# Column vectors through small TensorE transposes, filter loads into the Z tiles, a third hn buffer and late column sums in a spectral-gating and MLP block with its backward pass

## The chip, the cores and the metric

The kernel runs on one core of a Trainium2 chip. The metric is device time in microseconds (us). The engines are called PE (TensorE, with PEld for its weight loads), DVE (VectorE), ACT (ScalarE), POOL (GpSimd) and SP (SyncE); SP issues all of the kernel's DMAs, in its own program order.

## The reference

The reference computes one transformer-like block and, through its vector-Jacobian product, all its gradients. S = 2048 rows, D = 512 columns, F = 1792 hidden columns, bf16:

```python
mod = (silu(c) @ w_mod)           # sa, ca, ga, sb, cb, gb: six rows of 512
h = layernorm(x) * (1 + ca) + sa
x = x + ga * irfft2(rfft2(h) * (w_r + 1j * w_i))
h = layernorm(x) * (1 + cb) + sb
out = x + gb * (relu(h @ w1 + b1) ** 2 @ w2 + b2)
_out, _vjp = jax.vjp(_f, A_x, A_w_r, A_w_i, B_w1, B_b1, B_w2, B_b2, c, w_mod)
_grads = _vjp(grad_out)
```

The ten outputs are `out` (out_0) and the gradients of x (out_1), of the filter `w_r`, `w_i` (out_2, out_3; 2048 x 257 each), of w1 (out_4), b1 (out_5), w2 (out_6), b2 (out_7), c (out_8) and w_mod (out_9).

## The kernel before

Rows are held as 128 partitions by 16 row tiles `t` (four blocks `b` of four). The two-dimensional Fourier transforms are products with tables built on the chip: LF and LG (stored to DRAM and loaded again for the backward pass as LFb, LGb), Cf, CdF, CdB and TA. A spectrum is worked on in eight pairs `gi`, each a tile of 128 x (2, 2, 257).

The stages, in order of the program:

1. **Start.** x, c, w_mod and transposed loads of grad_out (gT) and w2 arrive. c lands as a 128 x 4 column tile `ccol` (L532) and b1 as a 128 x 14 column tile `b1colb` (L548); both are read from DRAM so that neighbouring elements of a partition lie 128 elements apart. Layernorm statistics, the first transform, the six modulation rows, the tables. In the background, `gaT = w2 · grad_out` (L640).
2. **Forward spectrum** (L656 to L672). `spec_f23` makes a pair's spectrum X; `ew_f` multiplies it with the filter pair (`Wt[gi]`, a ring of three tiles named W) into `Z[gi]` and stores X to `xs_dram`. `spec_g1` and `spec_g23` transform Z back.
3. **MLP forward and backward to its input** (`stage_g`, `stage_h`, `stage_o`, L721 to L854). `stage_h` makes h and gaT and stores both to DRAM (`h_dram`, `gh_dram`). `stage_o` makes the output rows, and the gradient rows `u` (two buffers), each stored to `gx1_dram` and transformed into UT for the backward spectrum. The gradient of b1, `gb1b`, a 128 x 14 column tile, is then written twice: to out_5 and to `gb1_dram` (L852 to L854), every element to its own place of 2 bytes.
4. **Backward spectrum** (L937 to L955). The same transforms; `ew_b` multiplies the gradient G with the filter (`Wb`, two buffers) into Z, and with the stored spectrum (`Xb`, two buffers) into gW, the filter's gradient (two buffers), which goes to out_2 and out_3. In `spec_f23` ACT copies one half of each AE tile and DVE the other (L357, L358).
5. **Rows of the gradient of x** (L962 to L1002). For each of the 16 row tiles: `spec_g23` on PE, copies on ACT, eight instructions on DVE, the store of `gx`. `n1b` and `gxb` bring four row tiles at a time. Two column sums on PE per row tile (L982 with `gh1`, L983 with `q1`) run four rows late (`Delayed(4)`).
6. **Weight gradients.** `grad_w1` (L888): seven transposed loads `ghn` from gh_dram (two buffers), 64 matmuls L900 for each, in groups of 16 that end in three DVE instructions (L903, L909, L912). `grad_w2` (L876): fourteen transposed loads `hn` from h_dram (two buffers), 16 matmuls L882 each. `GMod.emit` makes a row block of the gradient of w_mod; each call needs a load `wmc` (one buffer). The gradient of c, `gcb`, a 128 x 4 column tile, goes to out_8 (L1024), again 2 bytes to a place.

The order on each engine is set by the framework's scheduler from the order of the code and from priorities. `Priority(tc, LATE)` around grad_w1, grad_mod_mid and grad_w2 puts their instructions behind those of the later stage 5 where both could run, so that grad_w1 fills gaps of PE in stage 5 and runs alone behind it, and grad_w2 comes last. Each engine then takes its instructions in that fixed order, and so does SP with its DMAs: a DMA that has to wait holds back all that stand behind it on SP.

Of the kernel before, what the change touches and what calls it, by code (L numbers as in the profile page):

```python
# [9 lines left out]
AF = mybir.ActivationFunctionType  # L10
# [75 lines left out]
def build_ta(tc, K, constp, g, pspool):  # L86
# [17 lines left out]
    pst = pspool.tile([P, P], BF16, name="ta_ps")  # L104
# [218 lines left out]
def spec_f23(tc, K, UT, Cd, dc, dest, elementwise):  # L323

    nc = tc.nc
    with tc.tile_pool(name="aep", bufs=1) as aep, \
# [18 lines left out]
        for gi in range(8):  # L345
# [12 lines left out]
            nc.vector.tensor_copy(out=dst[:, 1], in_=src[:, 1])  # L358
# [99 lines left out]
def kernel(  # L458
# [92 lines left out]
    nc.vector.tensor_copy(ccolf, ccol)  # L551
# [8 lines left out]
    psF1 = tc.alloc_tile_pool(name="psF1", bufs=2, space=PSUM)  # L560
    psM = tc.alloc_tile_pool(name="psM", bufs=2, space=PSUM)
# [138 lines left out]
    with tc.tile_pool(name="psR", bufs=1, space=PSUM) as psR, tc.tile_pool(name="psO", bufs=2, space=PSUM) as psO_pool, \  # L700
# [151 lines left out]
        with nc.allow_non_contiguous_dma(reason="tiny"):  # L852
            nc.sync.dma_start(out5_view, gb1b)
            nc.sync.dma_start(gb1_dram.rearrange("(fc p) -> p fc", p=P), gb1b)  # L854
# [82 lines left out]
    with tc.tile_pool(name="f23b", bufs=2) as fr, tc.tile_pool(name="ewb", bufs=2) as ew:  # L937
        Wt, Xt = [], []
        for gi in range(8):
            Wt.append(fr.tile([P, 2, 2, FP], BF16, name="Wb"))  # L940
            nc.sync.dma_start(Wt[gi][:, :, 0, 0:DF], wr_view[:, pair_slice(gi), :])
            nc.sync.dma_start(Wt[gi][:, :, 1, 0:DF], wi_view[:, pair_slice(gi), :])
# [3 lines left out]
        def ew_b(gi, G):  # L946
            cmul(nc, ew, Wt[gi], G, Z[gi][:, :, 0, 0:DF], Z[gi][:, :, 1, 0:DF], True)
# [14 lines left out]
    with tc.tile_pool(name="fin", bufs=2) as fp, tc.tile_pool(name="psE", bufs=2, space=PSUM) as psE, \  # L962
# [3 lines left out]
        late = Delayed(4)  # L966
        for b in range(NB):
            n1b = fp.tile([P, TB, D], BF16, name="n1b")
            nc.sync.dma_start(n1b, n1_dram[:, TB * b:TB * b + TB, :])
            gxb = fp.tile([P, TB, D], BF16, name="gxb")  # L970
            nc.sync.dma_start(gxb, gx1_dram[:, TB * b:TB * b + TB, :])
            for j in range(TB):
                t = TB * b + j
                n1row = n1b[:, j, :]
                psY = spec_g23(tc, K, CS, t, fp, psE, psE)
                gh1 = fp.tile([P, D], BF16, name="gh1", bufs=6)
                nc.scalar.copy(out=gh1, in_=psY)
                q1 = fp.tile([P, D], BF16, name="q1", bufs=6)
                nc.vector.tensor_tensor(q1, gh1, n1row, op=ALU.mult)

                def sums(t=t, gh1=gh1, q1=q1):
                    nc.tensor.matmul(gsa_ps, lhsT=K["ones_col"], rhs=gh1, start=(t == 0), stop=(t == NT - 1))  # L982
                    nc.tensor.matmul(gca_ps, lhsT=K["ones_col"], rhs=q1, start=(t == 0), stop=(t == NT - 1), tile_position=(0, 32))  # L983

                late.add(sums)
                gn = fp.tile([P, D], BF16, name="gn")
                nc.vector.tensor_tensor(gn, gh1, modb[:, CA1_B, :], op=ALU.mult)
                rr = fp.tile([P, 4], FP32, name="rr")
                gs = fp.tile([P, D], BF16, name="gs")
                nc.scalar.activation(gs, gn, AF.Copy, scale=inv1[:, t:t + 1], accum_out=rr[:, 0:1])  # L990
                jk = fp.tile([P, D], BF16, name="jk1")
                nc.vector.scalar_tensor_tensor(out=jk, in0=gs, scalar=K["onef"], in1=n1row, op0=ALU.mult, op1=ALU.mult,  # L992
                                               accum_out=rr[:, 1:2])
                nc.vector.tensor_scalar(rr[:, 2:4], rr[:, 0:2], -1.0 / D, None, op0=ALU.mult)
                v = fp.tile([P, D], BF16, name="v")
                nc.vector.tensor_scalar(v, n1row, rr[:, 3:4], rr[:, 2:3], op0=ALU.mult, op1=ALU.add)
# [67 lines left out]
```

## Time and profile before

| | us |
|---|---|
| median of 3 runs | 629.2 |
| lowest and highest | 621.39 and 630.54 |
| the profiled execution | 626.75 |
| its span on the core | 624.9 |
| PE busy, of the span | 499.5 (80%) |
| DVE busy | 402.2 (64%) |
| ACT busy | 239.0 (38%) |
| mean granted clock of TensorE | 0.924 of full speed |

Times in the profile are microseconds from the start of the span. A row of the timeline gives the start, the busy time, the engine, the line, the operation, the output and the inputs, and in square brackets the idle time ahead of it with what ended that. A row of the table of stretches gives the stretch, its length, the busy time (and number) of PE, PEld, DVE, ACT and POOL, the granted clock of TensorE, the mean busy share of the 16 DMA engines and the GB/s that they moved. A row of a DMA issue gives output, input, count, KB of each and the median us from issue to landing. Busy times of matmuls are modelled ends of pipelined instructions, so rates are taken from start to start or over whole rows.

### The profile page before, as it was taken

To read this page: it belongs to the slowest core of one execution; us is meant where nothing else is said; L and a number is where in the kernel's file an instruction comes from. 1 tells how busy PE (TensorE), PEld (TensorE's weight loads), DVE (VectorE), ACT (ScalarE), POOL (GpSimd) and SP (SyncE) were. 2 spreads that over 40 slices of the span, in tenths; PEclk is the share of its full clock that TensorE was granted. 3 is DMA by queue.
4 is the path that set the end of the run, shared out by engine and by line. 5 is a ranking of instruction groups with operands and counts; after the bars stand their busy time and mean duration, and the time that the engine had idled before them with its cause. 6 is when DMAs were issued, how large, how long until landed. Compare 5 with 4: busy or idle time off the path is not lost.

```text
span 624.9 us, 8582 instructions
## 1 busy us (share of the span) xinstructions
PE 499.5 (80%) x2803; PEld 256.5 (41%) x2844; DVE 402.2 (64%) x1133; ACT 239.0 (38%) x415; POOL 30.1 (5%) x112
## 2 busy tenths in 40 slices
PE   0778999989879989899999409767796499987666
PEld 0523468633433333344443104435442288732222
DVE  5897977375695895783794224976489977645001
ACT  2656854454522352253451104324476222251000
POOL 3212000022000011000000000000000000000000
PEclk9799999999989999989999858888999599989769
DMA  8963677364864374564289877999984189489654
GB/s 304 205 199 131 195 158 199 108 198 140 224 206 144 102 250 152 149 210 150 69 285 179 32 163 242 261 217 233 226 249 140 53 179 184 81 235 258 51 102 111
DMA packets 168096, 108.96 MB, mean 174 GB/s; under 512 B 94322, under 2 KB 162164, under 8 KB 167156
## 3 DMA queue, kind: packets, MB, share of 16 engines
q1 hardware_dynamic: 168052, 108.42, 68.6%
q8 instruction: 22, 0.36, 0.2%
q14 instruction: 22, 0.18, 0.1%
HBM read 43.02 MB, written 44.92 MB: 141 GB/s over the span
## 4 chain that ended last, share of the span: by engine, by line
DMA 20%; PE 20%; DVE 12%; SPq 3%; issue 2%; ACT 0%; POOL 0%; DVEq 0%; ACTq 0%; POOLq 0%
DMA hn<-h_dram 7%; PE mm L900 5%; PE mm L882 5%; DMA gx_dram<-u 5%; DMA out_dram<-gW 3%; PE og L781 3%; PE mm L763 2%; DMA ghn<-gh_dram 2%; PE og L799 2%; SPq L895 2%; DVE p L408 1%; DVE gaT L770 1%; DVE p L409 1%; DMA Wb<-in_A_w_r_dram 1%; DVE jk L992 1%
## 5 line engine op out<-in xcount | busy, mean ns | idle before, releaser
L882 PE MATMUL mm<-g_sb,hn 128*128 128x512 bf16 x219 | 58.1, 421 | 19.4 <-DMA hn<-h_dram 19.0
L640 PE MATMUL mm<-gT,w2T 128*128 128x512 bf16 x217 | 54.4, 378 | 8.3 <-DVE gaT L643 5.7
L900 PE MATMUL mm<-ghn,n_sb 128*128 128x256 bf16 x448 | 54.6, 282 | 7.5 <-DVE gw L912 5.1
L781 PE MATMUL og<-w,h 128*128 128x512 bf16 x217 | 55.9, 386 | 3.6 <-DVE h L768 3.3
L763 PE MATMUL mm<-h2T,w 128*128 128x512 bf16 x220 | 57.0, 386 | 0.2
L900 PEld LDWEIGHTS <-n_sb 128*128 128x128 bf16 x448 | 44.7, 101 | 20.4 <-issue 11.7
L799 PE MATMUL og<-w1T,gaT 128*128 128x512 bf16 x218 | 51.5, 380 | 0.3
L765 ACT ACTIVATE r<-mm,b1col 128x512 bf16<-128x512 f32 x56 | 38.3, 687 | 30.5 <-DVE gaT L770 22.7
L882 PEld LDWEIGHTS <-hn 128*128 128x128 bf16 x224 | 22.7, 106 | 53.1 <-DMA hn<-h_dram 23.7
L770 DVE SCALAR_TENSOR_TENSOR gaT<-r,onef,gaT 128x512 bf16<-128x512 bf16 x56 | 41.8, 746 | 0.0
L885 DVE TENSOR_TENSOR gw<-mm,modb 128x512 bf16<-128x512 f32 x14 | 9.7, 690 | 47.9 <-PE mm L882 47.9
L640 PEld LDWEIGHTS <-w2T 128*128 128x128 bf16 x224 | 21.4, 97 | 37.2 <-issue 12.2
L781 PEld LDWEIGHTS <-h 128*128 128x128 bf16 x224 | 20.4, 98 | 30.4 <-DVE h L768 6.5
L390 PE MATMUL psT<-Cf,utcs 128*128 128x512 bf16 x123 | 32.6, 379 | 0.2
L763 PEld LDWEIGHTS <-w 128*128 128x128 bf16 x224 | 21.1, 99 | 25.0 <-issue 7.0
L799 PEld LDWEIGHTS <-gaT 128*128 128x128 bf16 x224 | 20.5, 98 | 25.9 <-issue 4.0
L375 PEld LDWEIGHTS <-Z 128*128 128x128 bf16 x256 | 26.2, 102 | 8.9 <-issue 4.7
L907 ACT ACTIVATE gtmp<-gb1bc,mcol 128x256 f32<-128x256 bf16 x28 | 14.1, 509 | 39.3 <-DVE gw L912 34.8
L643 DVE CAST gaT<-mm 128x512 bf16<-128x512 f32 x28 | 19.2, 687 | 14.3 <-PE mm L640 14.3
L807 DVE SCALAR_TENSOR_TENSOR u<-n2rows,rb,gb 128x512 bf16<-128x512 bf16 x16 | 12.0, 752 | 22.6 <-DMA gx_dram<-u 22.0
L801 ACT ACTIVATE cb<-og,inv 128x512 bf16<-128x512 f32 x16 | 11.0, 688 | 40.4 <-PE og L799 34.9
L452 DVE SCALAR_TENSOR_TENSOR gm_junk<-wmc,onef,gmbc 128x512 bf16<-128x512 bf16 x24 | 18.0, 749 | 9.3 <-DMA wmc<-in_w_mod_dram 6.3
(268 smaller groups left out, 858.3 us busy)
## 6 DMA issues: line engine op xcount, KB each, us to landing
h_dram<-h SPq DMA_DIRECT2D x56, 128.0 KB, 1.9
gh_dram<-gaT SPq DMA_DIRECT2D x56, 128.0 KB, 1.9
w<-in_B_w_dram SPq DMA_DIRECT2D x2, 1792.0 KB, 8.3
wm<-in_w_mod_dram SPq DMA_DIRECT2D x3, 1024.0 KB, 12.6
wmc<-in_w_mod_dram SPq DMA_DIRECT2D x6, 512.0 KB, 4.5
out_dram<-gwm SPq DMA_DIRECT2D x6, 512.0 KB, 4.2
xs_dram<-Xs SPq DMA_DIRECT2D x8, 257.0 KB, 5.0
Xb<-xs_dram SPq DMA_DIRECT2D x8, 257.0 KB, 5.4
```

The lines of the kernel that those rows point to most:

```text
L375: nc.tensor.matmul(ps[:, ch, :], lhsT=Z[gi][:, x, ri, f0:f0 + P], rhs=lg_window(K, g, e + ri), start=(n == 0), stop=(n == 3))
L390: nc.tensor.matmul(ps, lhsT=CS[:, t, c].rearrange("p r a b -> p (r a b)"), rhs=K["Cf"][:, c, :], start=(c == 0), stop=(c == 3))
L452: nc.vector.scalar_tensor_tensor(out=junk, in0=wmc[:, dc, :], scalar=K["onef"], in1=gmbc, op0=ALU.mult, op1=ALU.mult, accum_out=self.gsc[: ...
L640: nc.tensor.matmul(ps, lhsT=w2T[:, dc, fc * P:(fc + 1) * P], rhs=gT[b][:, dc, :], start=(dc == 0), stop=(dc == 3))
L643: nc.vector.tensor_copy(out=gaT[fc][:, b * SB:(b + 1) * SB], in_=ps)
L763: nc.tensor.matmul(ps, lhsT=w1[:, dc, fc * P:(fc + 1) * P], rhs=h2T[b][:, dc, :], start=(dc == 0), stop=(dc == 3))
L765: nc.scalar.activation(r, ps, AF.Relu, bias=b1col[:, fc:fc + 1])
L770: nc.vector.scalar_tensor_tensor(out=gaT[fc][:, sl], in0=r, scalar=K["onef"], in1=gaT[fc][:, sl], op0=ALU.mult, op1=ALU.mult, accum_out=gb ...
L781: nc.tensor.matmul(ps, lhsT=hT[b, fc][:, j * P:(j + 1) * P], rhs=w2[:, fc, :], start=(fc == 0), stop=False)
L799: nc.tensor.matmul(ps, lhsT=gaT[fc][:, t * P:(t + 1) * P], rhs=w1T[:, fc, :], start=(fc == 0), stop=(fc == NFC - 1))
L882: nc.tensor.matmul(ps, lhsT=hn[:, t, :], rhs=g_sb[:, t, :], start=(t == 0), stop=(t == NT - 1))
L900: nc.tensor.matmul(ps[:, 0:W4], lhsT=n2_sb[:, t, dc * P:(dc + 1) * P], rhs=ghn[:, t, :], start=(t == 0), stop=(t == NT - 1))
```

## The change

- **Columns.** c and b1 are loaded as rows of 128 elements into one 32 x 128 tile `vrow`, transposed by one PE transpose into PSUM, and copied from there to `b1col` and `ccolf`. The gradient of b1 (128 x 14) is transposed by PE to 14 x 128, copied by DVE to `gb1r`, and stored twice, 14 pieces of 256 bytes each. The gradient of c goes the same way as 4 x 128. Two PSUM pools are opened earlier for this.
- **Filter.** The W and Wb rings go. Each filter pair is loaded into the tile `Z[gi]` that later takes the product, and `cmul` reads it there and writes the product over it. All eight pairs have their own tile, so no load waits for a buffer of a ring.
- **AE copies.** In the backward spectrum (`dc is None`) ACT copies both halves.
- **hn** has three buffers.
- **Stage 5.** n1 and gx1 come one row tile at a time (`n1row`, `gxl`, three buffers each). `q1` is kept for all 16 row tiles in one tile, and the 16 column sums of q1 run in one loop behind the rows, with the lowest priority (`2 * LATE`). The lag of the others is 2. Some outputs are written over inputs (gn, gs).

```diff
@@ spec_f23
             nc.scalar.copy(out=dst[:, 0], in_=src[:, 0])
-            nc.vector.tensor_copy(out=dst[:, 1], in_=src[:, 1])
+            if dc is None:
+                nc.scalar.copy(out=dst[:, 1], in_=src[:, 1])
+            else:
+                nc.vector.tensor_copy(out=dst[:, 1], in_=src[:, 1])
@@ start
-    ccol = p0.tile([P, 4], BF16, name="ccol")
-    b1colb = p0.tile([P, NFC], BF16, name="b1colb")
-    with nc.allow_non_contiguous_dma(reason="tiny"):
-        nc.sync.dma_start(ccol, c.rearrange("b (dc p) -> p (b dc)", p=P))
+    vrow = p0.tile([32, P], BF16, name="vrow")
+    nc.vector.memset(vrow, 0.0)
+    nc.sync.dma_start(vrow[0:4, :], c.rearrange("b (dc p) -> (b dc) p", p=P))
+    nc.sync.dma_start(vrow[8:8 + NFC, :], B_b1.rearrange("(fc p) -> fc p", p=P))
...
-    with nc.allow_non_contiguous_dma(reason="tiny"):
-        nc.sync.dma_start(b1colb, B_b1.rearrange("(fc p) -> p fc", p=P))
-    nc.vector.tensor_copy(b1col, b1colb)
-
-    nc.vector.tensor_copy(ccolf, ccol)
...
+    pv = psM.tile([P, 32], BF16, name="vrow_ps", bufs=1)
+    nc.tensor.transpose(pv, vrow, K["ident"][0:32, 0:32])
+    nc.vector.tensor_copy(b1col, pv[:, 8:8 + NFC])
+    nc.vector.tensor_copy(ccolf, pv[:, 0:4])
@@ forward spectrum (the backward spectrum likewise, with Wb)
-        Wt = []
         for gi in range(8):
-            Wt.append(fr.tile([P, 2, 2, FP], BF16, name="W"))
-            nc.sync.dma_start(Wt[gi][:, :, 0, 0:DF], wr_view[:, pair_slice(gi), :])
-            nc.sync.dma_start(Wt[gi][:, :, 1, 0:DF], wi_view[:, pair_slice(gi), :])
+            nc.sync.dma_start(Z[gi][:, :, 0, 0:DF], wr_view[:, pair_slice(gi), :])
+            nc.sync.dma_start(Z[gi][:, :, 1, 0:DF], wi_view[:, pair_slice(gi), :])
...
-            cmul(nc, ew, X, Wt[gi], Z[gi][:, :, 0, 0:DF], Z[gi][:, :, 1, 0:DF], False)
+            cmul(nc, ew, X, Z[gi], Z[gi][:, :, 0, 0:DF], Z[gi][:, :, 1, 0:DF], False)
@@ gradient of b1
-        with nc.allow_non_contiguous_dma(reason="tiny"):
-            nc.sync.dma_start(out5_view, gb1b)
-            nc.sync.dma_start(gb1_dram.rearrange("(fc p) -> p fc", p=P), gb1b)
+        pg = psR.tile([NFC, P], BF16, name="pst2")
+        nc.tensor.transpose(pg, gb1b, K["ident"])
+        gb1r = constp.tile([NFC, P], BF16, name="gb1r")
+        nc.vector.tensor_copy(gb1r, pg)
+        nc.sync.dma_start(gb1_dram.rearrange("(fc p) -> fc p", p=P), gb1r)
+        nc.sync.dma_start(out_5.rearrange("(fc p) -> fc p", p=P), gb1r)
@@ grad_w2
-            hn = gwp.tile([P, NT, P], BF16, name="hn", bufs=2)
+            hn = gwp.tile([P, NT, P], BF16, name="hn", bufs=3)
@@ rows of the gradient of x
-        late = Delayed(4)
-        for b in range(NB):
-            n1b = fp.tile([P, TB, D], BF16, name="n1b")
-            nc.sync.dma_start(n1b, n1_dram[:, TB * b:TB * b + TB, :])
-            gxb = fp.tile([P, TB, D], BF16, name="gxb")
-            nc.sync.dma_start(gxb, gx1_dram[:, TB * b:TB * b + TB, :])
...
+        late = Delayed(2)
+        q1 = fp.tile([P, NT, D], BF16, name="q1", bufs=1)
+        for t in range(NT):
+            psY = spec_g23(tc, K, CS, t, fp, psE, psE)
+            gh1 = fp.tile([P, D], BF16, name="gh1", bufs=5)
+            nc.scalar.copy(out=gh1, in_=psY)
+            late.add(lambda t=t, gh1=gh1: nc.tensor.matmul(gsa_ps, lhsT=K["ones_col"], rhs=gh1, start=(t == 0), stop=(t == NT - 1)))
+            n1row = fp.tile([P, D], BF16, name="n1row", bufs=3)
+            nc.sync.dma_start(n1row, n1_dram[:, t, :])
+            gxl = fp.tile([P, D], BF16, name="gxl", bufs=3)
+            nc.sync.dma_start(gxl, gx1_dram[:, t, :])
+            nc.vector.tensor_tensor(q1[:, t, :], gh1, n1row, op=ALU.mult)
...
         late.flush()
+        with Priority(tc, 2 * LATE):
+            for t in range(NT):
+                nc.tensor.matmul(gca_ps, lhsT=K["ones_col"], rhs=q1[:, t, :], start=(t == 0), stop=(t == NT - 1),
+                                 tile_position=(0, 32))
@@ gradient of c
-        with nc.allow_non_contiguous_dma(reason="tiny"):
-            nc.sync.dma_start(out8_view, gcb)
+        pg = psX.tile([4, P], BF16, name="mm")
+        nc.tensor.transpose(pg, gcb, K["ident"])
+        gcr = fp.tile([4, P], BF16, name="gcr", bufs=1)
+        nc.vector.tensor_copy(gcr, pg)
+        nc.sync.dma_start(out_8.rearrange("b (dc p) -> (b dc) p", p=P), gcr)
```

The scheduler places the instructions anew. Line numbers in the pieces below are each kernel's own. SP at the end of stage 3, before; `gb1b` is the gradient of b1, LGb the table that the backward spectrum needs, `gx_dram<-u` the store of a gradient row:

```order
L813 DMA yl<-y_dram 128x512
L853 DMA out_dram<-gb1b 128x14x1
L854 DMA gb_dram<-gb1b 128x14x1
L684 DMA LGb<-LG_dram 128x7168
L790 DMA out_dram<-o_3883 128x512
L790 DMA out_dram<-o_3911 128x512
L810 DMA gx_dram<-u 128x512
```

SP at the same place now:

```order
L811 DMA yl<-y_dram 128x512
L682 DMA LGb<-LG_dram 128x7168
L788 DMA out_dram<-o_3877 128x512
L788 DMA out_dram<-o_3905 128x512
L808 DMA gx_dram<-u 128x512
L811 DMA yl<-y_dram 128x512
L682 DMA LGxb<-LGx_dram 128x1536
L808 DMA gx_dram<-u 128x512
L811 DMA yl<-y_dram 128x512
L808 DMA gx_dram<-u 128x512
L854 DMA gb_dram<-gb1r 14x128
L855 DMA out_dram<-gb1r 14x128
```

The two stores of the gradient of b1 have moved from ahead of the LGb load to behind the last but one gradient row.

SP where stage 5 begins, before (`gb1bc` is the gradient of b1 read back to all partitions, `ghn` a transposed load for grad_w1, n1b and gxb four row tiles of stage 5):

```order
L891 DMA gb1bc<-gb_dram 128x1792
L950 DMA out_dram<-gW 128x2x257
L951 DMA out_dram<-gW 128x2x257
L454 DMA out_dram<-gwm 128x4x512
L895 DMA_TRANSPOSE ghn<-gh_dram 128x16x256 x2
L969 DMA n1b<-n_dram 128x2048
L971 DMA gxb<-gx_dram 128x2048
```

SP at the same place now:

```order
L892 DMA gb1bc<-gb_dram 128x1792
L896 DMA_TRANSPOSE ghn<-gh_dram 128x16x256
L974 DMA n1row<-n_dram 128x512
L976 DMA gxl<-gx_dram 128x512
L974 DMA n1row<-n_dram 128x512
L976 DMA gxl<-gx_dram 128x512
L974 DMA n1row<-n_dram 128x512
L976 DMA gxl<-gx_dram 128x512
L442 DMA wmc<-in_w_mod_dram 128x4x512
L457 DMA out_dram<-gwm 128x4x512
L896 DMA_TRANSPOSE ghn<-gh_dram 128x16x256
```

One ghn load, not two, now stands ahead of the first rows' loads, and those are a quarter of the size.

SP in grad_w2, before (`hn` is its transposed load, gw a store of 128 rows of the gradient of w2, gcb the gradient of c):

```order
L886 DMA out_dram<-gw 128x512
L879 DMA_TRANSPOSE hn<-h_dram 128x16x128 x2
L1024 DMA out_dram<-gcb 128x4x1
L886 DMA out_dram<-gw 128x512
L879 DMA_TRANSPOSE hn<-h_dram 128x16x128
```

SP at the same place now:

```order
L880 DMA_TRANSPOSE hn<-h_dram 128x16x128
L887 DMA out_dram<-gw 128x512
L880 DMA_TRANSPOSE hn<-h_dram 128x16x128
L1021 DMA out_dram<-gcr 4x128
L880 DMA_TRANSPOSE hn<-h_dram 128x16x128
L887 DMA out_dram<-gw 128x512
```

The store of the gradient of c now stands behind the eleventh hn load of the kernel and has 4 rows; before it stood behind the ninth and had 512 single elements.

More of the change, by code (lines that the diff above doesn't have):

```diff
@@ L103, in build_ta @@
     nc.scalar.activation(TA, v, AF.Sin, scale=TWO_PI / 128, bias=K["npi"])
-    pst = pspool.tile([P, P], BF16, name="ta_ps")
+    pst = pspool.tile([P, P], BF16, name="ta_ps", bufs=1)
     nc.tensor.transpose(pst, TA, K["ident"])
@@ L965 @@
         gsa_ps, gca_ps = acc1[0:1, :], acc1[32:33, :]
-        late = Delayed(4)
-        for b in range(NB):
-            n1b = fp.tile([P, TB, D], BF16, name="n1b")
-            nc.sync.dma_start(n1b, n1_dram[:, TB * b:TB * b + TB, :])
-            gxb = fp.tile([P, TB, D], BF16, name="gxb")
-            nc.sync.dma_start(gxb, gx1_dram[:, TB * b:TB * b + TB, :])
[L972 to L996, printed above, removed]
-                v2 = fp.tile([P, D], BF16, name="v2")
-                nc.vector.tensor_tensor(v2, v, gs, op=ALU.add)
-                gx = fp.tile([P, D], BF16, name="gx")
-                nc.vector.tensor_tensor(gx, v2, gxb[:, j, :], op=ALU.add)
-                nc.sync.dma_start(out1_view[:, t, :], gx)
@@ new lines @@
+        late = Delayed(2)
[10 more added lines that the diff above has]
+            nc.vector.tensor_tensor(q1[:, t, :], gh1, n1row, op=ALU.mult)
+            gn = fp.tile([P, D], BF16, name="gn")
+            nc.vector.tensor_tensor(gn, gh1, modb[:, CA1_B, :], op=ALU.mult)
+            rr = fp.tile([P, 4], FP32, name="rr")
+            gs = fp.tile([P, D], BF16, name="gs")
+            nc.scalar.activation(gs, gn, AF.Copy, scale=inv1[:, t:t + 1], accum_out=rr[:, 0:1])
+            jk = fp.tile([P, D], BF16, name="jk1", bufs=1)
+            nc.vector.scalar_tensor_tensor(out=jk, in0=gs, scalar=K["onef"], in1=n1row, op0=ALU.mult, op1=ALU.mult,
+                                           accum_out=rr[:, 1:2])
+            nc.vector.tensor_scalar(rr[:, 2:4], rr[:, 0:2], -1.0 / D, None, op0=ALU.mult)
+            nc.vector.tensor_scalar(gn, n1row, rr[:, 3:4], rr[:, 2:3], op0=ALU.mult, op1=ALU.add)
+            nc.vector.tensor_tensor(gs, gn, gs, op=ALU.add)
+            gx = fp.tile([P, D], BF16, name="gx", bufs=3)
+            nc.vector.tensor_tensor(gx, gs, gxl, op=ALU.add)
+            nc.sync.dma_start(out1_view[:, t, :], gx)
```

15 lines of the change are left out of this document (6 added, 9 removed).

## The prediction

> **What bounds the kernel now.** I read the page first: the profiled execution took 626.75 us, its span is 624.9. No engine fills the span (PE 80%, DVE 64%), and the chain of work that ended last is led by transfers:
>
> ```profile
> DMA hn<-h_dram 7%; PE mm L900 5%; PE mm L882 5%; DMA gx_dram<-u 5%; DMA out_dram<-gW 3%; PE og L781 3%; PE mm L763 2%; DMA ghn<-gh_dram 2%; PE og L799 2%; SPq L895 2%; DVE p L408 1%; DVE gaT L770 1%; DVE p L409 1%; DMA Wb<-in_A_w_r_dram 1%;
> ```
>
> The table of waits prices two of them for the engine that waited (total, times, longest), and the timeline says what SP had issued just before (start, duration):
>
> ```profile
> DVE u L807 <- DMA gx_dram<-u: 22.0, 1, 22.0
> PE mm L882 <- DMA hn<-h_dram: 19.0, 8, 10.5
> 333.49 0.43 SPq L853 DMA_DIRECT2D out_dram<-gb1b  x1
> 334.86 1.81 SPq L854 DMA_DIRECT2D gb_dram<-gb1b  x1
> 336.77 2.06 SPq L684 DMA_DIRECT2D LGb<-LG_dram  x1
> 342.91 28.43 DMA gx_dram<-u
> 578.61 0.53 SPq L1024 DMA_DIRECT2D out_dram<-gcb  x1
> 588.79 10.61 SPq L879 DMA_TRANSPOSE hn<-h_dram  x1
> ```
>
> In both places a store of a column tile, 2 bytes to a place, stands ahead of a transfer that somebody waits for. Stall 1: a `u` store took 28.43 us. Stall 2: the 10.5 us wait for hn begins 10 us after `gcb`'s store. Whether bytes or pieces cost the time is told by the table of stretches, whose last two columns are DMA busy share and GB/s:
>
> ```profile
> 330.00:335.00 5.00, 5.00 (x24) 2.05 (x23) 1.09 (x3) 0.59 (x1) 0.00 (x0) 1.00 0.95 357
> 340.00:345.00 5.00, 4.93 (x26) 2.02 (x25) 3.62 (x8) 1.34 (x2) 0.00 (x0) 1.00 1.56 26
> 590.00:595.00 5.00, 0.00 (x0) 0.00 (x0) 0.00 (x0) 0.00 (x0) 0.00 (x0) 0.66 0.77 8
> LGb<-LG_dram SPq DMA_DIRECT2D x1, 1792.0 KB, 33.5
> gx_dram<-u SPq DMA_DIRECT2D x16, 128.0 KB, 1.8
> ```
>
> At 340 the queues are full while 26 GB/s move; ten microseconds earlier, as full, they moved 357. The median `u` store lands in 1.8 us. So pieces cost the time, and the transfers behind them wait. Bytes alone would put the 1792 KB of LGb at 5.1 us (at 357 GB/s).
>
> **The change part by part**, against 626.75.
>
> T1, gradient of b1. Its 2 x 1792 pieces go, and its 28 pieces of 256 bytes now stand behind the LGb load and all but the last `u`. The 22.0 us wait goes. PE, idle meanwhile, came back at half clock, seen in the first of two equal groups:
>
> ```profile
> 376.65 3.51 PE L350 MATMUL psB<-CdB,utcs 128*128 128x512 bf16 x8 [0.16 <-ACT utcs L320]
> 381.62 1.89 PE L350 MATMUL psB<-CdB,utcs 128*128 128x512 bf16 x8
> 15.06 0.29 PE L105 MATMUL ta_ps<-ident,TA 128*128 128x128 bf16 x1 [15.06 <-ACT TA L103]
> 3.59 0.17 DVE L551 CAST ccolf<-ccol 128x4 f32<-128x4 bf16 x1 [2.32 <-DMA ccol<-in_c_dram]
> ```
>
> That is 3.51 − 1.89 = 1.6 more. Added are one PE transpose and one copy, by the nearest rows 0.29 + 0.17 = 0.5 us, and I leave about 1 us for LGb's own 5.1 us, which the last `u` stores now queue behind. −22.0 − 1.6 + 0.5 + 1 = −22.1: **−22** (−24 if LGb is wholly covered, −19 if 4 us of it are not).
>
> T2, backward spectrum and the first rows:
>
> ```profile
> 376.65:443.20 66.55, 51.98 (x319) 33.77 (x323) 48.60 (x101) 24.93 (x45) 0.00 (x0) 0.87 0.98 241
> n_sb<-n_dram SPq DMA_DIRECT2D x1, 2048.0 KB, 9.1
> Xb<-xs_dram SPq DMA_DIRECT2D x8, 257.0 KB, 5.4
> 418.89 0.69 DVE L358 CAST AE<-psB 128x512 bf16<-128x512 f32 x1
> 434.87 11.81 SPq L895 DMA_TRANSPOSE ghn<-gh_dram  x2
> 444.47 0.82 PE L900 MATMUL mm<-ghn,n_sb 128*128 128x256 bf16 x6 [1.31 <-DMA ghn<-gh_dram]
> 451.63 0.76 DVE L979 TENSOR_TENSOR q<-gh,n1b 128x512 bf16<-128x512 bf16 x2 [2.35 <-DMA n1b<-n_dram]
> ```
>
> The DMA engines are 98% busy for 66.55 us, and the change takes no bytes from this stretch. It lets filter loads start early, since no ring holds them, but in SP's order `n_sb` still stands ahead of the last Xb loads. Eight AE copies leave DVE: 8 x 0.69 = 5.5 us, of 48.60 busy in a stretch whose end DMA sets; I count 1.5. ACT, 24.93 busy, has room. At the end one ghn load instead of two (11.81 us of SP together) stands ahead of the first rows, and the waits of 2.35 and 1.31 us and the 0.82 us of matmuls that ran ahead should go: 4.5. **−6** (−10 if all AE time counts; +4 if n_sb, 9.1 against 5.4 us for an Xb, now holds the last Xb back by its 3.7).
>
> T3, the rows and grad_w1:
>
> ```profile
> 446.86:494.65 47.79, 30.45 (x145) 12.33 (x146) 41.41 (x135) 29.21 (x67) 0.00 (x0) 0.84 0.59 171
> 481.86 0.75 DVE L992 SCALAR_TENSOR_TENSOR jk<-gs,onef,n1b 128x512 bf16<-128x512 bf16 x1
> 484.30 0.75 DVE L992 SCALAR_TENSOR_TENSOR jk<-gs,onef,n1b 128x512 bf16<-128x512 bf16 x1
> 520.66 14.15 PE L900 MATMUL mm<-ghn,n_sb 128*128 128x256 bf16 x128 [0.58 <-DVE gjk L909]
> L909 DVE SCALAR_TENSOR_TENSOR gjk<-mm,onef,w1n 128x256 bf16<-128x256 f32 x28 | 13.5, 484 | 13.5 <-PE mm L900 13.5
> 571.90 3.63 PE L882 MATMUL mm<-g_sb,hn 128*128 128x512 bf16 x16 [0.95 <-DMA hn<-h_dram]
> gxb<-gx_dram SPq DMA_DIRECT2D x4, 512.0 KB, 5.2
> ```
>
> DVE is the bound here (41.41 of 47.79); a row takes 2.44 us (481.86 to 484.30). On PE 112 of the 448 matmuls L900 now stand ahead of the last row's sums, before it was 48: 64 x 14.15/128 = 7.1 us less for the tail. Against it stand four more groups on DVE, 4 x 3 x 0.484 = 5.8 us, which its 47.79 − 41.41 = 6.4 idle can hold or not; and 16 column sums moved into PE-bound work, 16 x 3.63/16 = 3.6 us. A new wait: SP's third ghn load reuses the first one's buffer, so it waits for 64 matmuls, and the loads of rows 11 to 15 stand behind it. Its issue takes 11.81/2 = 5.9 us and a small transfer 1.8 (as for `u`), of which about one row, 2.44, is in hand: up to 5.3 lost. The sum lies between −7.1 + 3.6 = −3.5 and −7.1 + 3.6 + 5.8 + 5.3 = +7.6. **+2**, the middle. Smaller row loads carry the same bytes in a stage with DMA 59% busy: nothing. A page speaks against them: the Trainium skill, "DMA: Bandwidth & Descriptors", section "Rules for kernel authors", says to coalesce, because small transfers are mostly overhead, and its bandwidth section gives 138 GB/s at 64 KB. At that rate the 4 MB of row loads would take an estimated 30 us, still less than the stage, so by that page this term stands too; the 128 KB `u` stores that landed in 1.8 us point the same way.
>
> T4, grad_w2. Third buffer, and `gcb` stored in four pieces:
>
> ```profile
> hn<-h_dram SPq DMA_TRANSPOSE x14, 5.1
> 542.25:622.40 80.15, 59.76 (x233) 23.32 (x235) 22.72 (x53) 12.99 (x22) 0.00 (x0) 0.85 0.69 148
> 578.71 10.05 PE L882 MATMUL mm<-g_sb,hn 128*128 128x512 bf16 x31 [3.18 <-DMA hn<-h_dram]
> 580.00:585.00 5.00, 5.00 (x14) 1.86 (x13) 0.00 (x0) 0.00 (x0) 0.00 (x0) 0.52 0.20 28
> 599.28 10.00 PE L882 MATMUL mm<-g_sb,hn 128*128 128x512 bf16 x32 [10.53 <-DMA hn<-h_dram]
> 600.00:605.00 5.00, 5.00 (x13) 1.82 (x12) 0.00 (x0) 0.00 (x0) 0.00 (x0) 0.50 0.28 70
> ```
>
> PE waits 19.0 us for hn in eight waits: 10.53, 3.18 and six small ones, 5.3 together. After the two long ones the granted clock is 0.52 and 0.50. At 3.63/16 = 0.227 each, 31 matmuls take 7.0 us, not 10.05, and 32 take 7.3, not 10.00: 3.0 + 2.7 lost. 19.0 + 5.7 = 24.7. Of the small waits I let half stay, 2.7: **−22** (−25 if none stay; −16 if all stay and one cold group too). The new PE transpose of `gcb` stands in the middle of grad_w2's matmuls; were `gcb` late, all of them would queue behind it, one reason for the short end. By the Trainium skill, "TensorE: Matmul & The Clock Gate", section "Part 1: The HAM clock gate", the clock halves after an idle window of about 3.4 us and is back after about 3.4 us of work. By that the two groups would have lost an estimated 1.7 us each at most and the first, after 3.18 us, perhaps nothing, and the sum would be some 2 to 4 us less gain. Here the rows show half clock after 3.18 us, and for 5 us in the stretch at 600; they decide.
>
> T5, start. c's copy waited 2.32 us at 3.59, and PE starts at 15.06 on TA, not on c: the new load, transpose and copies lie in that cover. **0** (−2 to +1).
>
> Sum: −22 − 6 + 2 − 22 = −48. 626.75 − 48 = 578.75: **579 us**. The median of the runs is 629.2 and they spread by 1.5% (621.39 to 630.54), so the profiled execution stands for them, and about 2%, 12.6 us, is what a measurement can tell from no change.
>
> **The rivals.**
>
> R1: stall 1 is queueing behind LGb's own bytes and the stores beside it, and stays. Against it: 26 GB/s with full queues. Then the 22 us of T1 stay: 579 + 22 = 601. Chance 0.08.
>
> R2: grad_w2 is paced by the hn loads themselves. Each lands in 5.1 us and 16 matmuls take 3.63; if transposed loads do not overlap, a third buffer only moves the wait, and the eleven loads that are not there at the start each cost 5.1 − 3.63 = 1.47: 16 us. For it: the six small waits. Against it: those average 0.9 us with two buffers. 579 + 16 = 595. Chance 0.13.
>
> R3, on the other side: the row loads become the bound. Three rows in hand cover 3 x 2.44 = 7.3 us. They stand on SP between transposed loads and stores that wait for their own rows; where loads land later than 7.3 us, DVE waits every row, and at worst a load's 5.2 us (the gxb row) adds to each of 16: 83 us, 579 + 83 = 662. Against it: DMA 59% busy there. At half of that, 41: 620. Chance 0.05 for both, 0.02 at the long end.
>
> The forecast has the remaining 0.74.
>
> **How the numbers follow.** The predicted time is the forecast's. All low ends together give 626.75 − 24 − 10 − 3.5 − 25 − 2 = 562; all high ends 626.75 − 19 + 4 + 7.6 − 16 + 1 = 604, which will hardly meet. So the range runs from 562 to 601, where R1 ends; it holds R2, and leaves out R3, the corner above 601, and gains that no row shows. Faster by over 2% means below 616.6: forecast, R1 and R2 are (0.95); I keep 0.02 of that for mishaps with no row. Faster 0.93; within 2% 0.04 (R3 at half, part of the mishaps); slower 0.03.
>
> **What would show it.** T1: no wait of u L807 over 2 us, and 26 GB/s at full share nowhere in stage 3; R1 if the wait is still there. T2: the stretch of the backward spectrum still near 66 us at a share near 0.98. T3: at most one DVE wait for `n1row` or `gxl`, near row 11; R3 if there is one at each row. T4: waits for hn under 3 us in all, the clock near 1.0, and the stretch at 55 to 60 us, not 80.15; R2 if every group of 16 waits about 1.5 us. The prediction is wrong if grad_w2 stays above 65 us, or if the time freed in front comes back as DMA time in the backward spectrum.

## The result and the profile after

The changed kernel takes 584.4 us (median, 580.85 to 587.05), the kernel before in the same set 627.25 us (621.39 to 630.54): a ratio of 0.932, 95% interval 0.923 to 0.942. Forecast were 579 us, 562 to 601. The profiled executions, 626.75 and 585.71 us, differ by 41.0, so do their spans (624.9 and 583.9), and the traces can be laid beside each other stage by stage.

The chain of work that ended last is no longer led by transfers. From the page of the changed kernel, the lines that answer to those shown of before:

```profile
PE mm L901 5%; PE mm L883 5%; DMA ghn<-gh_dram 3%; DMA hn<-h_dram 2%; DMA n1row<-n_dram 2%; DVE gm_junk L455 1%; DVE jk L984 1%; DMA wmc<-in_w_mod_dram 1%; ACT gwm L454 1%; DVE gn L987 1%; DVE gx L990 1%; DVE gs L988 1%; DVE gn L979 1%; DVE gjk L910 0%; DVE gw L913 0%
L883 PE MATMUL mm<-g_sb,hn 128*128 128x512 bf16 x224 | 51.8, 388 | 2.9 <-DMA hn<-h_dram 2.9
```

The wait of `u` for its store is gone from the table of waits, and those of PE for hn fell from 19.0 us to 2.9. Where the 41 us were won is read from stretches between the same events of both kernels: the last `o` of stage 3, the last `u`, the first matmul of the backward spectrum (psB), the first `q` of stage 5, the first matmul of grad_w2, the end. The table of stretches of the kernel before (start and end, length, busy time and number of PE, PEld, DVE, ACT, POOL, granted clock, DMA share, GB/s):

```profile
338.90:374.10 35.20, 12.94 (x62) 5.10 (x62) 9.49 (x24) 3.83 (x6) 0.00 (x0) 0.74 0.88 89
376.70:451.60 74.90, 57.21 (x344) 36.21 (x349) 50.07 (x107) 30.16 (x55) 0.00 (x0) 0.89 0.99 238
451.60:542.20 90.60, 73.95 (x532) 51.13 (x534) 74.40 (x263) 37.34 (x80) 0.00 (x0) 0.89 0.64 156
542.20:624.90 82.70, 59.81 (x233) 23.36 (x236) 22.73 (x54) 12.99 (x22) 0.00 (x0) 0.86 0.67 145
```

and of the changed kernel:

```profile
341.40:356.10 14.70, 13.46 (x69) 5.33 (x66) 9.86 (x26) 3.71 (x6) 0.00 (x0) 1.00 0.57 198
358.40:425.20 66.80, 52.96 (x336) 34.92 (x336) 41.44 (x89) 29.80 (x56) 0.00 (x0) 0.90 0.97 234
425.20:523.10 97.90, 80.22 (x548) 53.34 (x548) 77.94 (x273) 40.43 (x88) 0.00 (x0) 0.90 0.76 173
523.10:583.90 60.80, 53.40 (x239) 22.28 (x236) 22.65 (x54) 12.88 (x22) 0.00 (x0) 0.97 0.79 188
```

| stretch | before | after | change | forecast |
|---|---|---|---|---|
| start to the last `o` (T5) | 338.9 | 341.4 | +2.5 | 0 |
| to the first psB (T1 without its cold group) | 37.8 | 17.0 | −20.8 | −20.4 |
| backward spectrum, to the first `q` (T2 and T1's 1.6 of cold clock) | 74.9 | 66.8 | −8.1 | −7.6 |
| rows and grad_w1, to grad_w2 (T3) | 90.6 | 97.9 | +7.3 | +2 |
| grad_w2, to the end (T4) | 82.7 | 60.8 | −21.9 | −22 |
| sum | | | −41.0 | −48 |

Two terms carry the difference, T3 and T5. T5 is not the change. In both kernels PE pauses at 180 us in stage 3 (busy 0.42 us of the 3 us before and 0.32 us after). PE waits for the same instruction of DVE, 3.34 us in both. Then the clock came back sooner in the kernel before; the stretches behind the pause, the first two of before, the other two of after:

```profile
183.00:186.00 3.00, 3.00 (x10) 0.95 (x9) 3.00 (x10) 1.37 (x2) 0.00 (x0) 0.60 0.65 217
186.00:189.00 3.00, 3.00 (x15) 1.17 (x13) 2.77 (x10) 1.38 (x2) 0.00 (x0) 1.00 0.67 218
```

```profile
183.00:186.00 3.00, 3.00 (x8) 0.88 (x7) 3.00 (x10) 1.37 (x2) 0.00 (x0) 0.50 0.63 209
186.00:189.00 3.00, 3.00 (x10) 1.05 (x8) 2.34 (x8) 0.69 (x1) 0.00 (x0) 0.55 0.71 230
```

At 186 to 189 us the granted clock is 1.00 in one and 0.55 in the other, 15 matmuls against 10. The first `o` row, a few us on, is 1.7 us later (added to x1 at 190.4 and 192.1 us). In another execution of the changed kernel (below) the pause was 3.34 us too, the clock was back at 1.00 in the stretch from 185.5 to 188.5 us, the first `o` row came at 190.1 us and the last at 338.0, both earlier than before. The other 0.8 us of T5 were not traced to a cause.

T3 is a loss in the rows. The stretch parts in two at the end of the last `gx`. The rows and what is left of grad_w1 behind them, two rows of before and two of after:

```profile
451.60:497.20 45.60, 30.06 (x145) 12.96 (x147) 43.11 (x142) 26.12 (x58) 0.00 (x0) 0.80 0.52 158
497.20:542.20 45.00, 43.90 (x389) 38.18 (x388) 31.29 (x122) 11.22 (x22) 0.00 (x0) 0.98 0.76 155
```

```profile
425.20:484.90 59.70, 44.25 (x225) 21.76 (x225) 51.73 (x172) 31.29 (x70) 0.00 (x0) 0.83 0.76 190
484.90:523.10 38.20, 35.97 (x325) 31.58 (x324) 26.21 (x102) 9.14 (x18) 0.00 (x0) 0.99 0.75 148
```

Behind the rows grad_w1 takes 6.8 us less, but the rows take 14.1 us more. DVE has 8.6 us more work in them (43.11 and 51.73) and is idle for 8.0 us where it was 2.5. The table of waits has, for the changed kernel (total, times, longest):

```profile
DVE q L977 <- DMA n1row<-n_dram: 6.0, 4, 2.3
```

SP, DVE and PE at row 11, from its timeline, in that order:

```profile
457.08 4.47 SPq L896 DMA_TRANSPOSE ghn<-gh_dram  x1
461.65 0.53 SPq L991 DMA_DIRECT2D out_dram<-gx  x1
462.23 0.42 SPq L974 DMA_DIRECT2D n1row<-n_dram  x1
...
464.74 0.42 DVE L977 TENSOR_TENSOR q<-gh,n1row 128x512 bf16<-128x512 bf16 x1 [2.27 <-DMA n1row<-n_dram]
467.15 0.42 DVE L977 TENSOR_TENSOR q<-gh,n1row 128x512 bf16<-128x512 bf16 x1 [1.25 <-DMA n1row<-n_dram]
...
467.62 0.38 PE L995 MATMUL acc<-q,ones_col 128*1 128x512 bf16 x1 [1.39 <-DVE q L977]
470.03 0.59 PE L995 MATMUL acc<-q,ones_col 128*1 128x512 bf16 x1 [2.03 <-DVE q L977]
473.35 3.57 PE L901 MATMUL mm<-ghn,n_sb 128*128 128x256 bf16 x16 [2.73 <-DVE gw L913]
482.09 17.60 PE L901 MATMUL mm<-ghn,n_sb 128*128 128x256 bf16 x144 [4.23 <-DVE gw L913]
```

The third ghn load is issued when the first one's 64 matmuls are done and holds SP for 4.47 us; `n1row` of row 11 stands behind it, and DVE waits 2.27 and 1.25 us for it and the next. The second ghn load, which held SP for 8.28 us from 425.66 on, does the same to row 3 (1.83 us). PE then waits for DVE: the late column sums for `q` (1.39 and 2.03), grad_w1's groups behind them for `gw` (2.73 and 4.23), 10.4 us in all. That is not the loss itself, for in the rows of before PE waited longer for the same two (12.0 and 5.1 us): DVE sets the pace of the rows in both kernels, and it has become slower.

### The profile page after: what moved, and what is told of

It reads as the page before. It is cut to its first block, busy times and chain, and to the rows that moved or that the text cites. A ratio compares the mean times of both kernels' runs of the same rounds, so it can differ in the third digit from the quotient of the medians.

```text
span 583.9 us, 8658 instructions
## 1 busy us (share of the span) xinstructions
PE 502.4 (86%) x2847; PEld 258.5 (44%) x2847; DVE 397.9 (68%) x1128; ACT 241.2 (41%) x423; POOL 30.3 (5%) x112
## 5 line engine op out<-in xcount | busy, mean ns | idle before, releaser
L640 PE MATMUL mm<-gT,w2T 128*128 128x512 bf16 x224 | 56.3, 386 | 7.7 <-DVE gaT L643 5.9
L779 PE MATMUL og<-w,h 128*128 128x512 bf16 x224 | 58.2, 392 | 3.3 <-DVE h L766 3.3
L761 PE MATMUL mm<-h2T,w 128*128 128x512 bf16 x224 | 59.0, 393 | 0.0
L901 PEld LDWEIGHTS <-n_sb 128*128 128x128 bf16 x448 | 45.1, 102 | 25.1 <-issue 14.8
L883 PE MATMUL mm<-g_sb,hn 128*128 128x512 bf16 x224 | 51.8, 388 | 2.9 <-DMA hn<-h_dram 2.9
L640 PEld LDWEIGHTS <-w2T 128*128 128x128 bf16 x224 | 21.9, 99 | 37.8 <-issue 13.5
L779 PEld LDWEIGHTS <-h 128*128 128x128 bf16 x224 | 20.8, 99 | 31.0 <-DVE h L766 6.0
L766 DVE TENSOR_TENSOR h<-r 128x512 bf16<-128x512 bf16 x56 | 23.6, 422 | 2.2 <-ACT r L763 2.2
```

Source lines behind the costliest of these rows:

```text
L640: nc.tensor.matmul(ps, lhsT=w2T[:, dc, fc * P:(fc + 1) * P], rhs=gT[b][:, dc, :], start=(dc == 0), stop=(dc == 3))
L761: nc.tensor.matmul(ps, lhsT=w1[:, dc, fc * P:(fc + 1) * P], rhs=h2T[b][:, dc, :], start=(dc == 0), stop=(dc == 3))
L766: nc.vector.tensor_tensor(h, r, r, op=ALU.mult)
L779: nc.tensor.matmul(ps, lhsT=hT[b, fc][:, j * P:(j + 1) * P], rhs=w2[:, fc, :], start=(fc == 0), stop=False)
L883: nc.tensor.matmul(ps, lhsT=hn[:, t, :], rhs=g_sb[:, t, :], start=(t == 0), stop=(t == NT - 1))
L901: nc.tensor.matmul(ps[:, 0:W4], lhsT=n2_sb[:, t, dc * P:(dc + 1) * P], rhs=ghn[:, t, :], start=(t == 0), stop=(t == NT - 1))
```

## The experiments

Eight runs, in two sets, put a part of the change into the kernel before or take one out of the changed kernel, and a third set times the changed kernel again beside three variants of it. Each set ran on one chip, and all had the kernel before beside them: 615.1, 613.1 and 616.6 us, where it was 627.25 at first. Ratios are to the kernel before of the same set. Stretches are those of the table, read in each run's own trace.

**The gradient of b1 alone**

```diff
-        with nc.allow_non_contiguous_dma(reason="tiny"):
-            nc.sync.dma_start(out5_view, gb1b)
-            nc.sync.dma_start(gb1_dram.rearrange("(fc p) -> p fc", p=P), gb1b)
+        pg = psR.tile([NFC, P], BF16, name="pst2")
+        nc.tensor.transpose(pg, gb1b, K["ident"])
+        gb1r = constp.tile([NFC, P], BF16, name="gb1r")
+        nc.vector.tensor_copy(gb1r, pg)
+        nc.sync.dma_start(gb1_dram.rearrange("(fc p) -> fc p", p=P), gb1r)
+        nc.sync.dma_start(out_5.rearrange("(fc p) -> fc p", p=P), gb1r)
```

> The kernel before with one part of the change: the gradient of b1 goes through a PE transpose and is stored as 2 x 14 pieces of 256 bytes (and one junk tile has one buffer, to make room). If the 2-byte pieces made the stall (term T1): the wait of u for its store goes, and the time falls by 20 to 22 us against the kernel before. If the stall was the bytes of LGb and of the stores beside it (R1): no change.

607.5 us, 0.988 of before (0.983 to 0.993): 7.6 us faster. Neither number came. The wait of `u` is gone, as the pieces theory has it, and the stretch from the last `o` to the last `u` is 14.6 us, as in the changed kernel. So the part works, but what it removes was smaller in this set than in the first profile.

**One column store instead of two** (the edit is against the run above)

```diff
-        nc.sync.dma_start(out_5.rearrange("(fc p) -> fc p", p=P), gb1r)
+        with nc.allow_non_contiguous_dma(reason="tiny"):
+            nc.sync.dma_start(out5_view, gb1b)
```

> As the run before, but only one of the two stores is by rows; the other is the 128 x 14 column store of 2-byte pieces, still ahead of the LGb load. If each piece has its price: about half of the stall stays, so the time is 9 to 12 us under the kernel before, and the u wait is about 10 us. If a column store has a fixed price, or only the second one is in the way: all of the stall stays or all goes. R1: no change.

610.2 us, 0.992 (0.990 to 0.995), 4.9 us under before and 2.7 over the run above. The `u` wait is back, at 7.0 us where about 10 was expected, and the store itself took 16.3 us; the row of the wait, and what the trace says of the tile `gb1b`:

```profile
DVE u L807 <- DMA gx_dram<-u: 7.0, 1, 7.0
...
DMA to landing us min/median/max: 16.3/16.3/16.3
```

**The changed kernel with both column stores back**

> The changed kernel with the two column stores of the gradient of b1 put back. Pieces theory: 20 to 22 us slower than the changed kernel, about 605 us, with the u wait back. If the change of order on SP, not the form of the store, was what helped: no difference to the changed kernel's 584.

The edit is the first diff the other way. 590.9 us, 0.961 (0.955 to 0.966). Against the ratio 0.943 of the changed kernel in the third set that is 1.8% of 615, about 11 us. The rows of the wait and of the load:

```profile
DVE u L806 <- DMA gx_dram<-u: 10.0, 1, 10.0
LGb<-LG_dram SPq DMA_DIRECT2D x1, 1792.0 KB, 21.7
```

From the last `o` to the last `u` it takes 14.6 us with no column store, 19.8 with one and 24.0 with two: 5.2 and 4.2 us each, a dose that goes with the stores. LGb lands in 21.7 us here and, without column stores, in 8.2 (first run). So the column stores ahead of LGb make stall 1, not LGb's bytes: R1 falls. Form and place were not taken apart here: in every run the scheduler set the column stores ahead of the LGb load and the row stores behind it, and a row store ahead of LGb was not tried. For the store of `gcb` they were (below, under two hn buffers). In the first profile the same two stores cost 20.6 us (35.2 − 14.6) and LGb took 33.5. What these stores of 2-byte pieces cost thus differs by a factor of two between the two profiled executions, of different sets; whether by the chip, the placement of the outputs or something else was not tried.

**The changed kernel with the column store of the gradient of c back**

```diff
-        pg = psX.tile([4, P], BF16, name="mm")
-        nc.tensor.transpose(pg, gcb, K["ident"])
-        gcr = fp.tile([4, P], BF16, name="gcr", bufs=1)
-        nc.vector.tensor_copy(gcr, pg)
-        nc.sync.dma_start(out_8.rearrange("b (dc p) -> (b dc) p", p=P), gcr)
+        with nc.allow_non_contiguous_dma(reason="tiny"):
+            nc.sync.dma_start(out8_view, gcb)
```

> The changed kernel with the 512-piece column store of the gradient of c put back; hn keeps three buffers. If the pieces alone made the stall in grad_w2: the 10.5 us wait returns, less one group of 16 matmuls (3.6 us) that the third buffer has in hand, plus up to 3 us of cold clock: 7 to 10 us slower than the changed kernel. If the third buffer is what cured it: no slower than 1 us.

595.1 us, 0.967 (0.961 to 0.974). Grad_w2 takes 76.0 us, 14.8 more than the 61.2 of the changed kernel in the third set, above the 7 to 10 that were expected. The row of the wait, SP's rows of the timeline, and two stretches of 2 us:

```profile
PE mm L884 <- DMA hn<-h_dram: 15.0, 3, 11.3
...
556.28 0.38 SPq L1019 DMA_DIRECT2D out_dram<-gcb  x1
556.76 17.92 SPq L881 DMA_TRANSPOSE hn<-h_dram  x2
...
562.00:564.00 2.00, 1.70 (x8) 0.59 (x6) 0.26 (x1) 0.00 (x0) 0.00 (x0) 1.00 0.66 20
568.00:570.00 2.00, 0.00 (x0) 0.00 (x0) 0.00 (x0) 0.00 (x0) 0.00 (x0) 0.50 1.48 15
```

Behind the 1 KB store SP spends 17.92 us on two transposed loads, and in the two stretches the DMA engines move 20 and 15 GB/s. The third buffer does not cover that.

**Two hn buffers**

```diff
-            hn = gwp.tile([P, NT, P], BF16, name="hn", bufs=3)
+            hn = gwp.tile([P, NT, P], BF16, name="hn", bufs=2)
```

> The changed kernel with two hn buffers instead of three. By term T4 the small waits for hn return: they were 5.3 us in the kernel before, now 2.9 are left, so 2 to 6 us slower than the changed kernel. If hn loads set the pace themselves (R2): no difference, since a third buffer only moves the wait. If the third buffer did most of T4: 10 us or more slower.

587.4 us, 0.960 (0.953 to 0.967). Grad_w2 takes 68.3 us, 7.1 more than 61.2; PE waits 5.7 us for hn, in nine waits, and 2.9 us for `gcb` at its transpose (in the third set's trace of the changed kernel it waits 3.4 us for hn and not for `gcb`). The third buffer and the store of `gcb` account for all of T4: 7.1 + 14.8 = 21.9. R2, by which a third buffer only moves the wait, falls. This run also takes form and place apart for `gcb`: its row store stands behind the ninth hn load, with two buffers, where the kernel before and the run of the gradient of b1 alone have the column store, and grad_w2 takes 68.3 us here against 82.7 and 83.6 there.

Rows and grad_w1 take 94.9 us in this run, though their code is the changed kernel's (97.1). With three buffers a third hn load stands on SP among the row loads; here there are two, and the waits for `n1row` are 2.4 us in all where the third set's trace of the changed kernel has 5.6. So part of T3 may be the price of the third hn buffer.

**The rows of before in the changed kernel**

```diff
-        late = Delayed(2)
-        q1 = fp.tile([P, NT, D], BF16, name="q1", bufs=1)
-        for t in range(NT):
+        late = Delayed(4)
+        for b in range(NB):
+            n1b = fp.tile([P, TB, D], BF16, name="n1b")
+            nc.sync.dma_start(n1b, n1_dram[:, TB * b:TB * b + TB, :])
+            gxb = fp.tile([P, TB, D], BF16, name="gxb")
+            nc.sync.dma_start(gxb, gx1_dram[:, TB * b:TB * b + TB, :])
+            for j in range(TB):
...
-        with Priority(tc, 2 * LATE):
-            for t in range(NT):
-                nc.tensor.matmul(gca_ps, lhsT=K["ones_col"], rhs=q1[:, t, :], start=(t == 0), stop=(t == NT - 1),
-                                 tile_position=(0, 32))
```

> The changed kernel with the row stage of before: n1 and gx1 four row tiles at a time, the column sums of q1 in the rows four rows late. Gradients written over inputs stay. If the lost 7 us of term T3 come from the third ghn load ahead of the loads of rows 11 to 15 and from the late sums, 5 to 8 us faster than the changed kernel, about 578. If they come from the four more groups of grad_w1 on DVE, which the order still interleaves: within 2 us of the changed kernel.

578.7 us, 0.946 (0.938 to 0.954). Its interval overlaps that of the changed kernel (0.938 to 0.947), so the times don't settle it. The traces say more: rows and grad_w1 take 94.0 us, against 97.1 in the third set's trace of the changed kernel. Of the 7.3 us of T3 this part returns about 3, as far as one trace each can say.

**The column sums back in the rows**

```diff
-            late.add(lambda t=t, gh1=gh1: nc.tensor.matmul(gsa_ps, lhsT=K["ones_col"], rhs=gh1, start=(t == 0), stop=(t == NT - 1)))
+            def sums(t=t, gh1=gh1):
+                nc.tensor.matmul(gsa_ps, lhsT=K["ones_col"], rhs=gh1, start=(t == 0), stop=(t == NT - 1))
+                nc.tensor.matmul(gca_ps, lhsT=K["ones_col"], rhs=q1[:, t, :], start=(t == 0), stop=(t == NT - 1),
+                                 tile_position=(0, 32))
+
+            late.add(sums)
...
-        with Priority(tc, 2 * LATE):
-            for t in range(NT):
-                nc.tensor.matmul(gca_ps, lhsT=K["ones_col"], rhs=q1[:, t, :], start=(t == 0), stop=(t == NT - 1),
-                                 tile_position=(0, 32))
```

> The changed kernel with the 16 column sums of q1 in the rows (two rows late) and the loads row by row as changed. If the late sums hold PE (it waited 3.4 us for q there): 2 to 4 us faster than the changed kernel. If the third ghn load is the cause, which still stands ahead of the loads of rows 11 to 15: within 2 us.

581.2 us, 0.951 (0.943 to 0.958), and 97.5 us for rows and grad_w1, as with the late sums (97.1). The place of the sums is worth nothing that shows.

**DVE copies half of each AE tile again**

```diff
-            if dc is None:
-                nc.scalar.copy(out=dst[:, 1], in_=src[:, 1])
-            else:
-                nc.vector.tensor_copy(out=dst[:, 1], in_=src[:, 1])
+            nc.vector.tensor_copy(out=dst[:, 1], in_=src[:, 1])
```

> The changed kernel with the second half of each AE tile of the backward spectrum copied by DVE again. The prediction counted 1.5 us of the 5.5 us as gain: 1 to 2 us slower than the changed kernel. If the stretch is set by the transfers alone: no difference. If DVE was the bound there: 5 us slower.

585.3 us, 0.955 (0.948 to 0.962). The backward spectrum takes 74.6 us, as in the kernel before (74.9), but rows and grad_w1 take 89.8, also as before (90.6). The two stretches, and SP's rows at their border:

```profile
359.50:434.10 74.60, 57.81 (x356) 36.37 (x357) 48.66 (x102) 27.89 (x50) 0.00 (x0) 0.91 0.98 239
434.10:523.90 89.80, 74.83 (x527) 50.56 (x527) 75.39 (x269) 39.37 (x85) 0.00 (x0) 0.94 0.69 164
...
410.09 9.18 SPq L893 DMA_TRANSPOSE ghn<-gh_dram  x1
420.45 6.39 SPq L893 DMA_TRANSPOSE ghn<-gh_dram  x1
428.19 0.37 SPq L971 DMA_DIRECT2D n1row<-n_dram  x1
```

With this edit the scheduler sets two ghn loads ahead of the first rows again, 9.18 and 6.39 us of SP. From the first psB to the last `gW` the backward spectrum takes 54.3 us here and 50.6 in the third set's trace of the changed kernel; from there to the first `q` it is 20.3 and 13.3. So of the 10.7 us between the two runs 3.7 lie in the spectrum itself, where the copies are, and 7.0 behind it, where the second ghn load now stands. Those 7.0 come back in rows and grad_w1, which are 7.3 us shorter here. A ghn load that stands ahead of the rows, or among them, is thus one thing seen twice, as a part of T2's gain and as T3's loss. Both stretches together take 164.4 us here and 161.0 there; some 3 us net belong to this edit, though by itself that is not clear of the 1 to 4 us by which equal stretches differ between executions.

**The changed kernel again, and three variants.** The first is the changed kernel itself.

> The changed kernel again, beside the others of this set. In the runs above the column stores cost 4.7 to 5.2 us each where they cost 10 in the first profile, and the kernel before took 613 to 615 us instead of 627. If that price is what differs, the changed kernel takes its 580 to 584 us again while the kernel before takes about 614: a ratio near 0.95. If all of the kernel runs faster there, about 572 and the ratio 0.932 again.

580.7 us; before 616.6; ratio 0.943 (0.938 to 0.947). The changed kernel differs by 3.7 us from its first timing, the kernel before by 10.7. Most of what the ratio lost is thus in the kernel before, by about the amount that the column stores cost less.

```diff
-    nc.sync.dma_start(g_sb, g_view)
...
+        nc.sync.dma_start(g_sb, g_view)
+
         def ew_b(gi, G):
```

> The changed kernel with the 2 MB load of g_sb (for grad_w2) put behind the filter loads in the code of the backward spectrum; before, it stood ahead of the first of them, for which DVE waits 9.9 us. If those bytes are the wait: it falls by about 5 to 6 us, and the time by as much. If the stretch is set by its bytes in all (DMA share 0.97), the bytes only move within it: no change, 2 us at most.

580.3 us, 0.941 (0.938 to 0.945): no change. The long wait for the first filter pair is gone, and another has come in its place. The first row is of the changed kernel of this set, the second of this variant:

```profile
DVE p L411 <- DMA Z<-in_A_w_i_dram: 9.8, 1, 9.8
```

```profile
DVE p L411 <- DMA Xb<-xs_dram: 6.6, 4, 4.6
```

The backward spectrum takes 63.2 us instead of 63.9, with a DMA share of 0.92 instead of 0.96. The bytes only moved within it, as the rival had it; that the bytes in all set its length fits this, but was not shown by itself.

The third run of this set has the rows of before and the later g_sb load together.

> The row stage of before in the changed kernel, with the g_sb load put behind the filter loads. If both gains are real and add: 5 us for the rows and 5 for the load, about 572 us. If the backward spectrum is set by its bytes: as with the old rows alone, about 578.

576.3 us, 0.935 (0.931 to 0.939), 4.4 us under the changed kernel of the same set, the fastest of all. The two intervals touch (0.939 and 0.938), so it is better by something under 1%. It lies between the two forecasts. Rows and grad_w1 take 90.2 us, against 97.1 and 94.0 with each edit alone; in SP's order the loads of the first eight rows now stand ahead of the first ghn load (issued from 415.05 and at 420.47 us), which neither edit does alone. The fourth run has the sums in the rows and deeper rings:

```diff
-            n1row = fp.tile([P, D], BF16, name="n1row", bufs=3)
+            n1row = fp.tile([P, D], BF16, name="n1row", bufs=7)
...
-            gxl = fp.tile([P, D], BF16, name="gxl", bufs=3)
+            gxl = fp.tile([P, D], BF16, name="gxl", bufs=7)
```

> The changed kernel with the column sums of q1 in the rows and seven buffers in place of three for the row loads, so that the third ghn load stands behind the loads of rows 11 to 14. If that ghn load and the short ring are what the row loads lost by: as fast as with the old rows, about 578. If one-row loads as such or the order of grad_w1 cost it: as with the sums in the rows alone, about 581.

578.5 us, 0.938 (0.934 to 0.942); the interval overlaps that of the changed kernel, so again the traces have to tell. The waits for `n1row` are gone from the table of waits, and from the first to the last row it takes 49.9 us instead of 58.6; grad_w1 behind them takes 43.6 instead of 38.5. Both together, 93.5 against 97.1, return 3.6 us, about what the rows of before return. So the ring of three with a ghn load in its way cost some 3 to 4 us, and most of what a faster row stage wins is lost again behind it, where fewer of grad_w1's matmuls have been done.

## Why the prediction was right

- **T4, −22, measured −21.9.** Right in its size and its causes. Its split was not given; it is 14.8 for the store of `gcb` and 7.1 for the third buffer. By the rows of the prediction it would be 13.2 (10.53 and 2.7 of cold clock) and 8.8, for the wait of 3.18 us ended as the store of `gcb` was issued (578.71 and 578.61 us) and cannot come from it; that the sum agrees to 0.1 us is luck. The clock part is seen too: 0.97 over the whole stretch, where it was 0.86.
- **T1, −22, measured −20.8 and the cold group.** Right in the first comparison, and the cause holds (one store, two stores, none), with form and place of the stores not taken apart. But the price of the stores was taken as a constant of the kernel. It halved in the later sets, and the part by itself was then worth 7.6 us. The prediction had no case for that; by the later sets' price its sum would have been some 11 us less.
- **T2, −6, measured −8.1 with 1.6 of cold clock.** Right in size and in its parts: to the last `gW` the stretch fell by 3.8 us (56.6 to 52.8), where 1.5 and the 1.6 of cold clock were counted, and from there to the first `q` by 4.3 (18.3 to 14.0), where 4.5 were. One trace each can't tell such parts to better than the 1 to 4 us above. And the two were treated as separate, while the ghn load moved because of the AE copies.
- **T3, +2, measured +7.3.** The wrong term, at the end of its own bounds. The step that failed is the choice of the middle between −3.5 and +7.6, by which the third ghn load and the four groups on DVE would be partly hidden. The gain came as counted: behind the rows grad_w1 takes 6.8 us less (7.1). The losses came nearly in full: the rows grew by 14.1 us, where 3.6 + 5.8 + 5.3 = 14.7 was the most, though not by the parts that were named. DVE's work grew by 8.6 and its idle time by 5.5, with 6.0 us of waits for `n1row` where row 11 and the next were expected to give up to 5.3 and gave 2.27 + 1.25; the place of the column sums, 3.6 in the sum, cost nothing that shows. Besides, T3 can't be read apart from T2: with one ghn load moved back ahead of the rows (DVE copies half of each AE tile again), the 7.3 us are gone and stand in the stretch before. How T3 divides among ghn load, ring of three and third hn buffer stays open.
- **T5, 0, measured +2.5**, of which 1.7 is a clock that came back late, in code that the change does not touch; the rest stays open.
- **The rivals.** R1 and R2 fell in the runs above. R3, row loads as the bound, came as a small part only: 6.0 us of waits for `n1row` in four rows, not sixteen.

Of the signs that were named, those for T1 (no 26 GB/s at full share), T2 (66 us at 0.97) and T4 (waits under 3 us) came as written; grad_w2 took 60.8 us to the end of the span, where 55 to 60 was given for a stretch that left out the last 2.5 us; and waits for `n1row` came in four rows, not one.

## What to carry to other kernels

Nobody waits for a small store of single elements, so its own row in a profile looks harmless; look at what stands behind it on the DMA queues and who waits for that, and send it through a transpose when it stands ahead of something needed. Where a scheduler places the rest anew, a gain in one stretch that reappears as a loss in the next is one load that has moved: add up both stretches before either is counted. And the length of such a stall is a number of one execution: here it was half as long in another set, so keep a case for that.

## What the runs showed of the hardware

- **What a column store costs the kernel does not go by its pieces.** One store of 1792 pieces of 2 bytes (3.5 KB) landed in 16.3 us and cost 5.2 us; one of 512 pieces (1 KB) cost 14.8 us, for behind it two transposed loads took 17.92 us to issue, at 20 and 15 GB/s in the stretches shown. The Trainium skill, "DMA: Bandwidth & Descriptors", section "Specifications", says that below 512 bytes the engines read, modify and write. No run here shows that step itself. In both tensors neighbouring 2-byte places are written from different partitions; whether that matters was not tried.
- **The same two stores cost 20.6 us in one set and 9.4 in another**, while the store of `gcb` stalled grad_w2 alike in both (82.7 us in the first profile, 83.6 in the run of the gradient of b1 alone, both with two hn buffers).
- **After an equal pause the clock came back at different times:** at 186 to 189 us it was 1.00 in one execution and 0.55 in another, after PE had waited 3.34 us in both. One such difference was worth 1.7 us here.
